# Four transfers by column quarter for the other branch's rows and the output rows

## The chip, the cores and the metric

The kernel runs on one core of a Trainium2 chip. The metric is device time in microseconds of one execution, from the timed runs. The engines are named as in the profile: PE (TensorE, with PEld for its weight loads), DVE (VectorE), ACT (ScalarE), POOL (GpSimd) and SP, the queue that issues nearly all transfers. Sixteen DMA engines move what SP issues.

## What is computed

The reference mixes two branches of one input x (2048 rows of 640) with a gate per row. Branch A goes through x in 64 segments of 32 rows; each carries a memory of 8 rows, which are the first 8 output rows of the attention of the segment before. Branch B is a gated feed-forward layer. Cut to what matters:

```python
for s in range(n_seg):                      # 64 segments, 32 heads of 192
    h = concatenate([mem, x_segment])       # 8 + 32 rows
    q, k, v = h @ Wq, h @ Wk, h @ Wv
    p = softmax(where(mask, q @ k.T * scale, -1e9))
    o = (p @ v) @ Wo
    mem = o[:, :8]; outs.append(o[:, 8:])
a = concatenate(outs)
b = (gelu(x @ w_gate) * (x @ w_up)) @ w_down
g = sigmoid((x * gate_w).sum(-1))
return g * a + (1 - g) * b
```

The memory makes the 64 segments a serial chain.

## The kernel before

The kernel has two stages. The first, up to about 185 us of the span, computes branch B in four blocks of 512 rows, writes its rows as bf16 to a scratch tensor in DRAM (`b_scr`), and loads most of branch A's weights into on-chip memory. The second, the chain, runs the 64 segments.

A segment is written as an ordered list of items (`PROG`): projections of q, k and v in groups (`g`), transposes, scores, softmax, the product with v, and the output projection (`wo`). The 32 heads are handled as four octets. The chain uses a shift: the 32 rows that a segment treats as its own are the 8 memory rows and 24 of x; the last 8 rows of x, the "left" rows, are worked on ahead in groups of four segments. A segment's output projection gives 32 rows, 24 output rows and the next memory. All 32 go through `mix` and are written by `out_store`; the last 8 places of each segment are written again by `outl_store`, with the left rows' results, which go through `mix_left` once in four segments. This makes s % 4 matter: the work on left rows differs between the four.

Not all weights fit on chip. Some pieces share a place with a partner (`partner`, `swap_in`), and in each segment 17 pieces are loaded over their partners (`swap_loads`, issued in `load_piece`, L597): in this order one Wk, four Wq, four Wk, five Wv and three Wo. Each waits on SP until PE has used the piece that stood there, and PE waits for each when it needs it. Of Wv and Wo they are those needed at the end of the segment.

The scheduler (`_Sched`) takes operations in program order and gives each engine its stream in that order. It knows which regions of memory, by bytes and partitions, an operation reads and writes, and puts a semaphore wait where an operation on another engine, or a transfer, has to be done first. A transfer adds 16 to its own semaphore when all of it has landed. An operation names a wait for every transfer that it directly depends on, unless its engine has already waited for that value.

In the chain all small transfers are on SP (`AUXQ = "sp"`), in order with the weight loads. In a segment SP issues: the nine Wk and Wq loads, four Wv loads, the store of the previous segment's output rows (`out_store`, L951), the load of the next x columns (`x_load`, L704), the fifth Wv load, three Wo loads, the load of the next q and k of left rows (L932), and then the load of branch B's rows for the current segment (`bz_load`, L942). Some segments add the load or the store of left rows (`bzl_load`, L947; `outl_store`, L956), of left x columns (L708), and the store of q and k of left rows (`left_store`, L893).

The buffer `bz` has 128 partitions of 160 elements: partitions 32j to 32j + 31 hold the 32 rows of column quarter j. There is one such buffer. `bz_load` fills it, `mix` multiplies it by 1 - g on GpSimd (L968) and adds g times the branch A result on VectorE (L970), and `out_store` writes it out in the next segment. So `bz_load` waits until `out_store` has landed, and `mix` waits for `bz_load`.

The left rows' buffer `bzl` is laid out the same way, and already goes in four transfers by column quarter:

```python
def bzl_load(g):
    for j in range(4):
        S_.add(AUXQ, lambda e, j=j: e.dma_start(bzl[32 * j:32 * j + 32], rows(b_scr, g)[1][:, :, DJ * j:DJ * (j + 1)]),
               reads=..., writes=[r_bzlj[j]], dma_sem="bzl%d" % j, name="bzl load g%d" % g)
```

At the end SP waits for all stores (`emit_final_waits`).

Of the kernel before, what the change touches and what calls it, by code (L numbers as in the profile page):

```python
# [231 lines left out]
def _build(nc, A_x, A_mem0, A_Wq, A_Wk, A_Wv, A_Wo, seg_len, w_gate, w_up, w_down,  # L232
           gate_w, out, opts=None):
# [5 lines left out]
    L = int(seg_len)  # L239
# [3 lines left out]
    DJ = Dm // 4  # L243
# [23 lines left out]
    S_ = _Sched(nc)  # L267
    Rg = S_.region
    AUXQ = opts.get("auxq", "act")

    x2 = A_x[0]
    out2 = out[0]
    b_scr = nc.dram_tensor("ffn_b_scratch", (S, Dm), BF, kind="Internal").ap()
# [63 lines left out]
    wsB_off = {}  # L337
# [14 lines left out]
    def bview(o, nbytes, plo=0, phi=128):  # L352
        return arena[plo:phi, o // 2:(o + nbytes) // 2]
# [4 lines left out]
    def sreg(o, nbytes, plo=0, phi=128):  # L358
        return Rg("sb", o, o + nbytes, plo, phi)
# [57 lines left out]
    bz, bzl = [bview(wsB_off[nm], DJ * 2) for nm in ("bz", "bzl")]  # L417
# [4 lines left out]
    zsum = fview(wsB_off["rows"], DJ * 4)  # L422
    r_zp = sreg(wsB_off["rows"], 2 * DJ * 4)
    r_bz, r_bzl = [sreg(wsB_off[nm], DJ * 2) for nm in ("bz", "bzl")]
    r_Z = [Rg("z", i, i + 1) for i in range(2)]
    mem0r = bview(wsB_off["uTl"], Dm * 2)
    r_mem0r = sreg(wsB_off["uTl"], Dm * 2)
# [206 lines left out]
    def load_residents(cls, pick=lambda key: True):  # L634
        for key in first:
# [7 lines left out]
           reads=[r_ident], writes=[r_ident])  # L643
    def asel(ap, reg, pattern, base, cm, fill):
# [12 lines left out]
           reads=[r_elw], writes=[r_elw])  # L657
# [19 lines left out]
    for h in range(NH):  # L677
        for w_, sb_, rw_, nm in ((w_gate, wg_sb, r_wg, "wg"), (w_up, wu_sb, r_wu, "wu")):
            S_.add("sp", lambda e, h=h, w_=w_, sb_=sb_: e.dma_start(
                sb_[h], w_.rearrange("(p k) f -> p k f", p=128)[:, :, FH * h:FH * (h + 1)]),  # L680
                writes=[rw_[h]], dma_sem="%s%d" % (nm, h))
# [179 lines left out]
    AUXQ = "sp"  # L861
# [48 lines left out]
    for n, (g, o) in enumerate(units):  # L910
# [7 lines left out]
        if g == 0:  # L918
            S_.add("pool", lambda e, o=o, b=b: e.tensor_copy(out=stg[:, o], in_=lst[b][:, 0]), reads=[r_lst[b]], writes=[r_stg[o]],
                   name="stg s0 o%d" % o)  # L920
# [18 lines left out]
               name="Kl s%d o%d" % (s, o))  # L939

    def bz_load(s):
        S_.add(AUXQ, lambda e: e.dma_start(bz, b_scr[L * s:L * s + L, :].rearrange("t (j n) -> j t n", j=4)),  # L942
               reads=[Rg("dr", 128 * (s // 4), 128 * (s // 4) + 128)], writes=[r_bz], dma_sem="bz", name="bz load s%d" % s)

    def bzl_load(g):
        for j in range(4):
# [1 line left out]
                   reads=[Rg("dr", 128 * g, 128 * g + 128)], writes=[r_bzlj[j]], dma_sem="bzl%d" % j, name="bzl load g%d" % g)  # L948

    def out_store(s):  # L950
        S_.add(AUXQ, lambda e: e.dma_start(out2[L * s:L * s + L, :].rearrange("t (j n) -> j t n", j=4), bz),  # L951
               reads=[r_bz], writes=[Rg("do%d" % j, s, s + 1) for j in range(4)], dma_sem="outs", watch=True, name="out s%d" % s)

    def outl_store(g):
        for j in range(4):
# [309 lines left out]
    def segment(s):  # L1265
# [3 lines left out]
        for n, item in enumerate(PROG):  # L1269
            kind, i = item[0], item[1]  # L1270
            if kind == "g":
# [8 lines left out]
                if kind == "k" and i == 1:  # L1280
                    if s > 0:
                        out_store(s - 1)
                    if s + 1 < NSEG:
                        x_load(s + 1)
# [44 lines left out]
            if n == nqkv:  # L1329
                bz_load(s)  # L1330
                if q == 2:
                    bzl_load(g)
                if q == 1 and g + 2 < NG:
                    xl_load(g + 2)
# [22 lines left out]
    for s in range(NSEG):  # L1357
        segment(s)
    out_store(NSEG - 1)
    outl_store(NG - 1)  # L1360

# [28 lines left out]
def bass_gated_mix__memory_aug_recurrent_mem_tr__glu_gated_geglu__prompt_kernel(  # L1390
    nc,
    A_x,
    A_mem0,
    A_Wq,
    A_Wk,
    A_Wv,
    A_Wo,
    A_seg_len,
    B_x,
    B_w_gate,  # L1400
    B_w_up,
    B_w_down,
    gate_w,
    out,
):
    _build(nc, A_x, A_mem0, A_Wq, A_Wk, A_Wv, A_Wo, A_seg_len, B_w_gate, B_w_up, B_w_down, gate_w, out)
# [33 lines left out]
```

## Time and profile before

| what | value |
|---|---|
| three timed runs | 1785.28, 1790.60, 1790.21 us (median 1790.21) |
| span of the profiled execution | 1783.4 us |
| other time of that execution | none is given |
| PE busy | 1629.5 us, 91% of the span |
| DVE, ACT, POOL busy | 957.7, 793.8, 319.8 us |
| moved by DMA | 524.33 MB, mean 294 GB/s |
| share of the 16 DMA engines, SP's queue | 79.5% |
| granted clock of TensorE | 0.998 |

The span is the time from the first to the last instruction on the core. A line of the profile names the source line, the engine, the operation and output<-input. Waits are told as "who waited <- for whom: us in total, times, longest". A timeline line has start, duration, engine, line, and in brackets the idle time before it and what ended it. A transfer is issued by SP ("SPq") in some tenths of a microsecond and lands later; it has landed for its users when the last DMA engine that carries part of it is done.

### The profile page before, as it was taken

The numbers are of one execution on the slowest core, as the hardware profiler recorded it, in microseconds if no ns is written. First come the engines' busy times: TensorE is split into PE (matmuls) and PEld (weight loads), VectorE is DVE, ScalarE is ACT, GpSimd is POOL, SyncE is SP. The second block draws the span as 40 slices with busy tenths as digits, with TensorE's granted clock in tenths as the row PEclk, the third lists the DMA queues.
The fourth block names the chain that finished last, engine by engine and source line by source line (L and its number), as shares of the span: only waits on it lengthen the run. The fifth ranks groups of instructions, "written<-read, shape, count | busy, mean of one in ns | idle before, by whom it ended". The sixth has DMA issues, their size and how long they took to land.

```text
span 1783.4 us, 80070 instructions
## 1 busy us (share of the span) xinstructions
PE 1629.5 (91%) x39162; PEld 817.9 (46%) x31501; DVE 957.7 (54%) x2932; ACT 793.8 (45%) x1835; POOL 319.8 (18%) x1099
## 2 busy tenths in 40 slices
PE   9999989899998999899899999899999989899987
PEld 4554444454444444454444444454444444454443
DVE  2223555555555655555565655555555655555554
ACT  3222444444444444444444444444444544444443
POOL 1100111111211111111111111111211111111211
PEclk9999999999999999999999999999999999999999
DMA  9815887888788887888788887888888887888786
GB/s 332 297 45 177 329 318 266 324 322 316 289 295 298 318 311 261 318 318 315 287 299 299 311 319 263 322 310 319 298 299 300 317 290 269 321 313 321 289 303 260
DMA packets 263390, 524.33 MB, mean 294 GB/s; under 512 B 97384, under 2 KB 116224, under 8 KB 263040
## 3 DMA queue, kind: packets, MB, share of 16 engines
q1 hardware_dynamic: 259912, 516.11, 79.5%
q8 instruction: 276, 4.52, 1.0%
q10 hardware_dynamic: 3128, 3.09, 0.5%
q14 instruction: 74, 0.61, 0.1%
HBM read 498.00 MB, written 21.11 MB: 291 GB/s over the span
## 4 chain that ended last, share of the span: by engine, by line
PE 69%; DMA 13%; DVE 8%; ACT 6%; issue 4%; SPq 0%; DVEq 0%; ACTq 0%
PE ps L1039 20%; PE ps L226 15%; PE ps L1201 8%; DMA arena<-in_A_Wv_dram 7%; PE ps L1172 3%; DMA left_qk_scratch<-arena 3%; PE ps L802 3%; PE ps L799 3%; PE ps L882 3%; DVE arena L889 3%; PE ps L1093 2%; PE ps L817 2%; ACT arena L887 2%; PE ps L1080 2%; PE ps L1088 2%
## 5 line engine op out<-in xcount | busy, mean ns | idle before, releaser
L1039 PE MATMUL ps<-arena 128*32 128x384 bf16 x9940 | 734.8, 328 | 58.5 <-DVE arena L1344 40.4
L226 PE MATMUL ps<-arena 128*32 128x384 bf16 x7680 | 584.4, 326 | 10.8 <-ACT arena L887 6.1
L1039 PEld LDWEIGHTS ps<-arena 128*32 128x32 bf16 x9940 | 254.0, 96 | 420.1 <-issue 244.4
L1073 DVE STREAM_TRANSPOSE arena<-arena 128x384 bf16<-128x384 bf16 x512 | 279.0, 564 | 227.0 <-ACT arena L1059 226.6
L1059 ACT ACTIVATE arena<-ps 128x384 bf16<-128x384 f32 x512 | 236.2, 489 | 176.3 <-PE ps L1039 164.4
L1201 PE MATMUL ps<-arena 128*32 128x320 bf16 x6144 | 297.0, 300 | 16.1 <-issue 15.5
L1201 PEld LDWEIGHTS ps<-arena 128*32 128x32 bf16 x6144 | 163.6, 97 | 75.7 <-issue 26.5
L1119 ACT ACTIVATE ps<-ps 104x160 f32<-104x160 f32 x256 | 74.3, 290 | 236.4 <-DVE ps L1109 236.4
L1107 DVE TENSOR_REDUCE arena<-ps 104x4 f32<-104x160 f32 x256 | 83.1, 325 | 176.0 <-PE ps L1093 175.7
L1157 ACT ACTIVATE arena<-ps 128x448 bf16<-128x448 f32 x192 | 104.8, 546 | 143.3 <-PE ps L1144 143.3
L1191 POOL COPY arena<-arena 128x96 bf16<-128x96 bf16 x256 | 68.4, 267 | 522.6 <-ACT arena L1183 419.3
L936 POOL COPY arena<-arena 128x96 bf16<-128x96 bf16 x256 | 70.0, 274 | 498.7 <-PE ps L1093 436.3
L1183 ACT ACTIVATE arena<-ps 128x480 bf16<-128x480 f32 (+1 forms) x256 | 138.1, 540 | 34.0 <-PE ps L1174 29.0
L1062 ACT ACTIVATE arena<-ps 128x384 bf16<-128x384 f32 x256 | 124.8, 488 | 52.7 <-PE ps L1039 52.4
L1172 PE MATMUL ps<-arena 128*64 128x160 bf16 x1536 | 122.1, 243 | 10.4 <-issue 3.4
L1172 PEld LDWEIGHTS ps<-arena 128*64 128x64 bf16 x1536 | 80.6, 109 | 97.9 <-ACT arena L1157 46.6
L882 PE MATMUL ps<-arena 128*32 128x384 bf16 x1280 | 111.1, 330 | 1.2 <-issue 1.2
L1174 PE MATMUL ps<-arena 128*64 128x64 bf16 x1536 | 105.1, 194 | 5.8 <-issue 5.8
L1121 DVE TENSOR_REDUCE arena<-ps 104x4 f32<-104x160 f32 x256 | 81.8, 320 | 51.6 <-ACT ps L1119 43.9
L889 DVE STREAM_TRANSPOSE arena<-arena 128x384 bf16<-128x384 bf16 x128 | 73.8, 577 | 57.4 <-ACT arena L887 52.6
L1224 PE MATMUL ps<-arena 128*32 128x160 bf16 x3072 | 77.1, 234 | 22.2 <-DMA arena<-in_A_Wo_dram 12.6
L887 ACT ACTIVATE arena<-ps 128x384 bf16<-128x384 f32 x128 | 62.4, 490 | 67.6 <-DVE arena L889 38.5
(84 smaller groups left out, 1816.7 us busy)
## 6 DMA issues: line engine op xcount, KB each, us to landing
arena<-in_A_Wk_dram SPq DMA_DIRECT2D x335, 384.0 KB, 7.7
arena<-in_A_Wv_dram SPq DMA_DIRECT2D x335, 384.0 KB, 9.4
arena<-in_A_Wq_dram SPq DMA_DIRECT2D x272, 384.0 KB, 5.6
arena<-in_A_Wo_dram SPq DMA_DIRECT2D x205, 480.0 KB, 7.4
left_qk_scratch<-arena SPq DMA_DIRECT2D x64, 192.0 KB, 2.6
arena<-left_qk_scratch SPq DMA_DIRECT2D x63, 192.0 KB, 7.8
ffn_b_scratch<-arena ACTq DMA_DIRECT2D x16, 160.0 KB, 3.7
arena<-ffn_b_scratch SPq DMA_DIRECT2D x64, 40.0 KB
```

Of the source, the lines that this page charges most:

```text
L226: return e.add_instruction(mybir.InstMatmult(name=nm, start_tensor_calc=like["start"], stop_tensor_calc=stop, tile_size=(128, 32), tile_po ...
L882: fns.append(lambda e, outp=outp, rhs=rhs, j=j: e.matmul(outp, lhs, rhs, start=(k == 0), stop=(k == KT - 1), tile_position=(0, 32 * j)))
L889: S_.add("dve", lambda e: e.transpose(out=dst[:, :, m].rearrange("p q c i -> p c q i"), in_=rowl.rearrange("p (c r) -> p c r", r=L)), read ...
L1039: fns.append(lambda e, outp=outp, rhs=rhs, j=j: e.matmul(outp, lhs, rhs, start=(k == 0), stop=(k == KT - 1), tile_position=(0, 32 * j)))
L1059: S_.add("act", lambda e, m=m, bk=bk: e.activation(out=rows_sb[m], in_=ps[:, bk, 0:384], func=ACTF.Copy), reads=[r_ps[bk]], writes=[r_rows ...
L1062: S_.add("act", lambda e, i=i, bk=bk: e.activation(out=v_sb[i % NVB].rearrange("p (c n) -> p c n", c=3), in_=ps[:, bk, 0:384].rearrange("p ...
L1073: S_.add("dve", lambda e: e.transpose(out=dst[:, :, 0:L], in_=rows_sb[m].rearrange("p (c r) -> p c r", r=L)), reads=[r_rows[m]], writes=[r ...
L1157: S_.add("act", lambda e: e.activation(out=PT, in_=ps[:, bank, 0:PTW + 128], func=ACTF.Copy), reads=[r_ps[bank]], writes=[r_PT], name="pT ...
L1172: return [lambda e: e.matmul(full, v[:, e0:e0 + 64], PTm[:, i], start=True, stop=False, tile_position=(0, 64 * i), skip_group_check=True), ...
L1174: lambda e: e.matmul(part, vl[:, e0:e0 + 64], PTl[:, i], start=False, stop=True, tile_position=(0, 64 * i), skip_group_check=True)]
L1183: S_.add("act", lambda e: e.activation(out=apx(u[:, 0, 0, :], [[R, na], [3 * R, 4], [1, R]]), in_=ps[:, A, 0:na * W].rearrange("p (c t r) ...
L1201: fns.append(lambda e, i=i, t=t, j=j, gv=gv: e.matmul(ps[32 * j:32 * j + 32, bank, 0:2 * DJ].rearrange("p (h n) -> p h n", h=2), lhs2[i], ...
```

## The change

The load of branch B's rows and the store of the output rows were one transfer each, over all four column quarters: the DRAM side was walked as quarter, row, column. They become four transfers each, one per quarter, with 32 rows of 160 elements on both sides. Each of the four has a region of its own (32 partitions) and a semaphore of its own, so each load waits for the store of its own quarter alone. The bytes and the rows are the same.

```diff
+    r_bzj = [sreg(wsB_off["bz"], DJ * 2, 32 * j, 32 * j + 32) for j in range(4)]
...
     def bz_load(s):
-        S_.add(AUXQ, lambda e: e.dma_start(bz, b_scr[L * s:L * s + L, :].rearrange("t (j n) -> j t n", j=4)),
-               reads=[Rg("dr", 128 * (s // 4), 128 * (s // 4) + 128)], writes=[r_bz], dma_sem="bz", name="bz load s%d" % s)
+        for j in range(4):
+            S_.add(AUXQ, lambda e, j=j: e.dma_start(bz[32 * j:32 * j + 32], b_scr[L * s:L * s + L, DJ * j:DJ * (j + 1)]),
+                   reads=[Rg("dr", 128 * (s // 4), 128 * (s // 4) + 128)], writes=[r_bzj[j]], dma_sem="bz%d" % j,
+                   name="bz load s%d" % s)
...
     def out_store(s):
-        S_.add(AUXQ, lambda e: e.dma_start(out2[L * s:L * s + L, :].rearrange("t (j n) -> j t n", j=4), bz),
-               reads=[r_bz], writes=[Rg("do%d" % j, s, s + 1) for j in range(4)], dma_sem="outs", watch=True, name="out s%d" % s)
+        for j in range(4):
+            S_.add(AUXQ, lambda e, j=j: e.dma_start(out2[L * s:L * s + L, DJ * j:DJ * (j + 1)], bz[32 * j:32 * j + 32]),
+                   reads=[r_bzj[j]], writes=[Rg("do%d" % j, s, s + 1)], dma_sem="outs%d" % j, watch=True, name="out s%d" % s)
```

The order of instructions on all engines stays as it was; SP issues eight transfers in place of two per segment. In the built program `mix`'s multiply on GpSimd waits on the four load semaphores in place of one, and its second part on VectorE, which named none of them before, names all four.

## The prediction

> **What bounds the kernel now.** I read the page first, then the waits of TensorE, the waits and the timeline of the DMA-issuing queue SP in one segment, then VectorE and GpSimd at the segment's end. The page:
>
> ```profile
> span 1783.4 us, 80070 instructions
> PE 1629.5 (91%) x39162; PEld 817.9 (46%) x31501; DVE 957.7 (54%) x2932; ACT 793.8 (45%) x1835; POOL 319.8 (18%) x1099
> PE 69%; DMA 13%; DVE 8%; ACT 6%; issue 4%; SPq 0%; DVEq 0%; ACTq 0%
> arena<-ffn_b_scratch SPq DMA_DIRECT2D x64, 40.0 KB
> ```
>
> PE carries the chain, DMA comes second with 13%. The load to be split (last line) moves only 40 KB, 64 times. The waits of PE's weight loads say which transfers PE waits for (total us, times, longest):
>
> ```profile
> PEld ps L1039 <- DMA arena<-in_A_Wv_dram: 22.2, 36, 1.8
> PEld ps L1224 <- DMA arena<-in_A_Wo_dram: 17.6, 24, 1.1
> PEld ps L1039 <- DMA arena<-in_A_Wk_dram: 12.1, 25, 1.0
> ```
>
> They are the swapped weight pieces. SP's timeline in a segment with s % 4 = 2 (start, us, line):
>
> ```profile
> 834.73 2.13 SPq L597 DMA_DIRECT2D arena<-in_A_Wv_dram  x4
> 836.90 0.57 SPq L951 DMA_DIRECT2D out_dram<-arena  x1
> 837.52 1.30 SPq L704 DMA_DIRECT2D arena<-x_scratch  x1
> 838.86 0.79 SPq L597 DMA_DIRECT2D arena<-in_A_Wv_dram  x1
> 842.62 2.18 SPq L597 DMA_DIRECT2D arena<-in_A_Wo_dram  x3
> 844.85 0.43 SPq L932 DMA_DIRECT2D arena<-left_qk_scratch  x1
> 847.08 0.55 SPq L942 DMA_DIRECT2D arena<-ffn_b_scratch  x1
> ```
>
> The stretch 835.5 to 847.9 of it (busy us of PE, PEld, DVE, ACT, POOL; last two columns: share of the 16 DMA engines, GB/s):
>
> ```profile
> 835.50:847.90 12.40, 11.15 (x290) 5.91 (x254) 7.65 (x24) 6.87 (x17) 1.87 (x7) 1.00 1.03 402
> ```
>
> All 16 engines are full in that stretch, and a 384 KB load takes 0.43 us to issue but about 1 us to move. Loads therefore stand in line: the fifth Wv load lands 9.3 us after its issue (median), the third Wo load 8.0. What counts for PE is the engine that finishes last, not SP's time of issue. In the trace I compared the last landing of the third Wo piece with the first weight load that waits for it: they are under 0.2 us apart in 29 of 63 segments, all with s % 4 = 1 or 2. In the others PE comes 0.2 to 2.6 us later.
>
> **The change, part by part.** (1) The store's time in the DMA engines. The last store of the run stands alone; the stretch 1778 to 1780 in forty slices:
>
> ```profile
> GB/s 0 0 0 0 0 0 0 0 0 0 0 0 13 38 58 77 77 77 77 83 77 77 77 70 19 0 0 0 164 0 0 0 0 0 0 0 0 0 0 0
> DMA packets 133, 0.05 MB, mean 25 GB/s; under 512 B 132, under 2 KB 132, under 8 KB 132
> ```
>
> That is 128 rows of 320 B and 4 completions at a flat 77 GB/s, where a full queue moved 402: one such transfer uses 4 of the 16 engines and holds them 40 KB / 77 GB/s = 0.53 us. Its DRAM pattern begins with the 4 column quarters, and the trace has 4 landings for it; the x load (L704), whose patterns begin with 128 rows, has 16. The new ones begin with 32 rows on both sides, and I take them by the x load: each engine gets 2 rows of each, 8 in all, 0.53 / 4 = 0.13 us, and four completions. The four old engines gain, the other twelve carry new work ahead of the fifth Wv load and the Wo loads. Lower end 0.13 us (completions free); upper end from the 10 KB loads of L947, whose last landings are 0.19 us apart where their 8 rows per engine take 0.13, so 0.06 for each further transfer: 0.13 + 4 x 0.06 = 0.37. I take 0.18, near the low end, because the completions are only 4-byte packets that the trace gives 9 ns each. It counts only where the last engine is among the twelve. The store's own four landings tell: they end a median of 0.9 us before the last landing of the x load queued right behind it, and are within 0.25 us of it in 6 of 64. So the last engine is nearly always another, and 29 segments pay: 29 x 0.18 = 5.2 us (ends 29 x 0.13 = 3.8 and 29 x 0.37 = 10.7). The Wv waits fall in the same segments and add nothing.
>
> A rule of the Trainium skill bears on this: "DMA: Bandwidth & Descriptors", "Why a DMA increments its semaphore by 16 and not by 1", says that a transfer uses the largest number of engines up to 16 that divides the slowest dimension of both its patterns. By it 4 and 128 give 4 now, and 32 and 32 give 16. The trace agrees for before (the quarter share above); no run shows the after yet. That page's "Rules for kernel authors" speak against a split: of two transfers to separate partition halves they say "Don't bother", since the parts share the same engines. By it the change gains nothing and the time is 1790 at best; no run here shows it yet.
>
> (2) SP's issues: six more per segment. A small transfer takes 0.43 (L932), 0.55 (L942), 0.58 (L951) or 0.60 us (L947), so with 0.04 between them three more are 1.4 to 1.9 us; I take 1.8. After the store they push the x load, the fifth Wv load and, if SP is still busy, Wo. Ahead of Wo SP idles 2.8 to 2.9 us (medians in segments 1 and 2, least 1.4), and the two pushed loads stand 5 us in line, so the cost is nothing; without the line each would land 1.8 us later. GpSimd's x copy comes 1.3 us after that load's landing; 0.2 is hidden.
>
> (3) The b load at the segment's end. SP already waits there for the store:
>
> ```profile
> SPq L942 <- DMA out_dram<-arena: 72.1, 44, 3.0
> ```
>
> The store will end with the last of 16 engines, not of 4: 0.9 + 0.2 us later, then 1.8 for issues. Behind it stand the bzl or left-x loads, then the next segment's q/k store and Wk, Wq loads. SP idles before these 5.8, 6.0, 3.5 and 8.4 us (s % 4 = 0, 1, 2, 3), 2.5 at the least; 2.8 is covered, barely so in one class. Where b is needed:
>
> ```profile
> 828.43 0.69 POOL L968 TENSOR_SCALAR arena<-arena 128x160 bf16<-128x160 bf16 x1 [0.81 <-DMA arena<-ffn_b_scratch]
> 830.31 0.32 POOL L936 COPY arena<-arena 128x96 bf16<-128x96 bf16 x1 [1.19 <-DVE arena L1344]
> 830.17 0.34 DVE L970 SCALAR_TENSOR_TENSOR arena<-arena 128x160 bf16<-128x160 bf16 x1
> 832.18 0.58 DVE L1073 STREAM_TRANSPOSE arena<-arena 128x384 bf16<-128x384 bf16 x1 [1.67 <-ACT arena L1059]
> ```
>
> By the line of queued loads b lands 0.5 to 1 us later. GpSimd's multiply ends 1.05 us before VectorE uses it at 830.17, and VectorE then has 1.67 us idle; GpSimd's next copy has 1.19 us and is read by the scores at 833.28. Cost nothing; without cover, at most 1 us in 64 segments.
>
> (4) More waits: mix1 on GpSimd waits on four b semaphores rather than one, mix2 on VectorE on four it did not name before. mixl1 (L976) has four such waits and starts 0.16 us after its predecessor, mix1 0.13 with one. Hidden in the same idle time.
>
> (5) The tail. The last stores of left rows start at 1780.02, on the landing of the store of 1777.41. Four issues put the last quarter's landing some 1.3 us later; the last of the four left stores waits for it, and now issues at 1780.8. Between 0 and 0.9, I take 0.5.
>
> **Sum.** 5.2 + 0.5 = 5.7 us. The profiled execution's span of 1783.4 becomes 1789.1. The page gives no other time of it; it is 1.9 us under the fastest timed run and 6.8 under the median, and I add the same 5.7 to the median: 1790.2 + 5.7 = 1796 (0.32%).
>
> **Rivals.** *SP becomes late.* Place: the end of segments with s % 4 = 2, 16 of them, with 3.5 us of cover. The store's later end takes 1.1, so it decides once a new issue takes over 0.76 us. The x load's reached 1.30 in the lines above, and 1.75 at most, for it; the rows of 0.43 to 0.60 speak against. At 1.0 each SP is 3 x 1.04 + 1.1 - 3.5 = 0.7 us late: 11 us more, 1807. *The four engines were the brake.* If the last landing is on one of the four, it moves forward by 0.53 - 0.18 = 0.35 us: 29 x 0.35 = 10 us, 1780. It decides where one of them ends more than 0.18 us after every other. For it: all four carry both small transfers, the bzl and outl quarters too. Against: the landing order in (1). *Hidden.* If PE's delay of 0.18 us is taken back by a later wait, or the new transfers hold four engines as the old ones do, 1790 to 1791. For it: half the segments have over 0.2 us to spare; against: the third Wo piece feeds the last matmuls before the next segment's rows.
>
> **How the numbers follow.** Forecast 0.50, SP late 0.22, four engines 0.14, hidden 0.14. About 0.3% (5.4 us) is what a measurement can tell from no change. The forecast's own range is 1794 to 1801, two thirds of it over 1795.6: slower 0.33 + 0.22 = 0.55; same 0.17 + 0.13 = 0.30; faster 0.14 + 0.01 = 0.15. The range runs from 1782, inside the four engines' case, to 1810, past SP's price at 1.0 us; some 0.15 is outside.
>
> **What would show it.** Right: the third Wo load's landing 0.2 us later against its issue order, PE's waits on Wo some 5 us more in total, GpSimd's wait for b longer without PE's waits on L1344 growing. SP's rows for the new transfers should read 0.43 to 0.6; at 0.8 or more the first rival holds, and PE's waits on Wk and Wq grow. If Wo and Wv waits shrink, the four engines were the brake. Wrong outright: new transfers that still hold only some engines.

## The result, and the profile after

The changed kernel took 1799.08 us (median of 20 runs), the kernel before 1789.99 us beside it: a ratio of 1.0039 by the means of the runs, interval 1.0024 to 1.0053, or +7.0 us (4.3 to 9.5; the medians alone are 9.1 us apart). A second comparison on another chip gave 1.0052 (1.0038 to 1.0066), +9.3 us. The forecast was +5.7 us, with "slower" as the likeliest outcome. The size holds; the way to it holds only in part.

The page after, on the lines shown of before, and the line of SP's queue (packets, MB, share of the DMA engines), whose line of before stands last:

```profile
span 1795.2 us, 80668 instructions
PE 1635.5 (91%) x39181; PEld 815.8 (45%) x31501; DVE 963.4 (54%) x2932; ACT 794.6 (44%) x1835; POOL 319.8 (18%) x1099
q1 hardware_dynamic: 267592, 516.14, 79.5%
PE 63%; DMA 19%; DVE 8%; ACT 5%; issue 4%; SPq 1%; DVEq 0%; ACTq 0%; POOL 0%; POOLq 0%
q1 hardware_dynamic: 259912, 516.11, 79.5%
```

The engines execute the same instructions, and DMA has gone from 13% to 19% of the chain. VectorE is busy 5.7 us longer; 3.6 us of it are mix's second part, whose mean went from 0.348 to 0.404 us. SP's queue has 267592 - 259912 = 7680 packets more. All are 4-byte completions: 64 segments x 2 transfers x (4 x 16 in place of 4). So each new transfer uses all 16 engines, which was an assumption. It is what the Trainium skill, "DMA: Bandwidth & Descriptors", "Why a DMA increments its semaphore by 16 and not by 1", gives for 32 rows on both sides.

PE's waits for the weights (lines moved by 1 to 4 in the changed file: L1039 is L1043, L1224 is L1228):

```profile
PEld ps L1043 <- DMA arena<-in_A_Wv_dram: 26.1, 49, 1.8
PEld ps L1043 <- DMA arena<-in_A_Wk_dram: 23.9, 48, 1.9
PEld ps L1228 <- DMA arena<-in_A_Wo_dram: 21.3, 27, 1.2
```

Wo has 3.7 us more, as forecast in kind. Wk, at 12.1 before, has 11.8 us more, which was not forecast (another pair of profiles, below, does not repeat it). SP's timeline where s % 4 = 2:

```profile
836.83 2.35 SPq L598 DMA_DIRECT2D arena<-in_A_Wv_dram  x4
839.22 2.87 SPq L955 DMA_DIRECT2D out_dram<-arena  x4
842.13 0.42 SPq L705 DMA_DIRECT2D arena<-x_scratch  x1
842.60 0.43 SPq L598 DMA_DIRECT2D arena<-in_A_Wv_dram  x1
844.92 1.28 SPq L598 DMA_DIRECT2D arena<-in_A_Wo_dram  x3
846.25 1.28 SPq L933 DMA_DIRECT2D arena<-left_qk_scratch  x1
849.83 1.72 SPq L944 DMA_DIRECT2D arena<-ffn_b_scratch  x4
...
856.05 0.38 SPq L894 DMA_DIRECT2D left_qk_scratch<-arena  x1
```

The four stores of this segment took longer than most: 2.87 us, where the median is 2.10. Even so SP has idle time ahead of the Wo loads and of the q/k store, so SP did not become the bound here. What did change is in VectorE's waits (before, then after):

```profile
DVE arena L970 <- POOL arena L968: 0.6, 2, 0.4
DVE arena L974 <- POOL arena L972: 21.1, 32, 2.5
```

Mix's second part on VectorE, which waited for GpSimd 0.6 us in total before, waits 21.1 us in 32 segments. One of these segments has s % 4 = 0. First VectorE, GpSimd and SP of it after the change, from their timelines:

```profile
1005.87 0.29 DVE L1348 STREAM_TRANSPOSE arena<-arena 128x96 bf16<-128x96 bf16 x1
1007.20 0.47 DVE L974 SCALAR_TENSOR_TENSOR arena<-arena 128x160 bf16<-128x160 bf16 x1 [1.03 <-POOL arena L972]
1007.59 0.57 DVE L890 STREAM_TRANSPOSE arena<-arena 128x384 bf16<-128x384 bf16 x1
...
1006.38 0.68 POOL L972 TENSOR_SCALAR arena<-arena 128x160 bf16<-128x160 bf16 x1 [1.72 <-DMA arena<-ffn_b_scratch]
...
1008.18 0.39 SPq L894 DMA_DIRECT2D left_qk_scratch<-arena  x1
1008.61 0.50 SPq L598 DMA_DIRECT2D arena<-in_A_Wk_dram  x1
```

Then a segment of the same kind in the kernel before:

```profile
804.38 0.29 DVE L1344 STREAM_TRANSPOSE arena<-arena 128x96 bf16<-128x96 bf16 x1
804.60 0.34 DVE L970 SCALAR_TENSOR_TENSOR arena<-arena 128x160 bf16<-128x160 bf16 x1
804.86 0.57 DVE L889 STREAM_TRANSPOSE arena<-arena 128x384 bf16<-128x384 bf16 x1
...
805.46 0.38 SPq L893 DMA_DIRECT2D left_qk_scratch<-arena  x1
805.89 0.50 SPq L597 DMA_DIRECT2D arena<-in_A_Wk_dram  x1
```

From the start of the last transpose of the memory rows to the first Wk load it takes 1.5 us before and 2.7 us after. The segment of before is typical; that of after is one of the three latest of its kind, with the q/k store 2.0 us behind the transposes' end where the median is 1.0. GpSimd waits for b; VectorE's mix waits for GpSimd; the transposes of the left rows stand behind mix on VectorE; the store of their q and k waits for these; and on SP the next segment's Wk and Wq loads stand behind that store. That chain became theory M. The forecast's own step, the store's extra time on every DMA engine, is theory E.

### The profile page after: what moved, and what is told of

It reads as the page before. It is cut to its first block, busy times and chain, and to the rows that moved or that the text cites. A ratio compares the mean times of both kernels' runs of the same rounds, so it can differ in the third digit from the quotient of the medians.

```text
span 1795.2 us, 80668 instructions
## 1 busy us (share of the span) xinstructions
PE 1635.5 (91%) x39181; PEld 815.8 (45%) x31501; DVE 963.4 (54%) x2932; ACT 794.6 (44%) x1835; POOL 319.8 (18%) x1099
## 3 DMA queue, kind: packets, MB, share of 16 engines
q1 hardware_dynamic: 267592, 516.14, 79.5%
## 4 chain that ended last, share of the span: by engine, by line
PE 63%; DMA 19%; DVE 8%; ACT 5%; issue 4%; SPq 1%; DVEq 0%; ACTq 0%; POOL 0%; POOLq 0%
PE ps L1043 18%; PE ps L226 13%; PE ps L1205 7%; DMA arena<-in_A_Wk_dram 6%; DMA left_qk_scratch<-arena 5%; DMA arena<-in_A_Wv_dram 5%; PE ps L800 3%; PE ps L803 3%; PE ps L1176 3%; DVE arena L890 2%; PE ps L818 2%; PE ps L1097 2%; PE ps L883 2%; DMA arena<-in_A_Wo_dram 2%; PE ps L1228 2%
## 5 line engine op out<-in xcount | busy, mean ns | idle before, releaser
L1043 PE MATMUL ps<-arena 128*32 128x384 bf16 x9940 | 737.3, 329 | 63.5 <-DVE arena L1348 39.6
L1043 PEld LDWEIGHTS ps<-arena 128*32 128x32 bf16 x9940 | 253.3, 96 | 436.7 <-issue 246.5
L1205 PE MATMUL ps<-arena 128*32 128x320 bf16 x6144 | 292.8, 299 | 12.4 <-issue 12.2
L1228 PE MATMUL ps<-arena 128*32 128x160 bf16 x3072 | 77.6, 234 | 25.8 <-DMA arena<-in_A_Wo_dram 15.8
```

What stands on the lines that cost most here:

```text
L1043: fns.append(lambda e, outp=outp, rhs=rhs, j=j: e.matmul(outp, lhs, rhs, start=(k == 0), stop=(k == KT - 1), tile_position=(0, 32 * j)))
L1205: fns.append(lambda e, i=i, t=t, j=j, gv=gv: e.matmul(ps[32 * j:32 * j + 32, bank, 0:2 * DJ].rearrange("p (h n) -> p h n", h=2), lhs2[i], ...
L1228: S_.add("pe", [lambda e, j=j, c=c, g_=g_, p=p: e.matmul(ps[32 * j:32 * j + 32, OB2, SC:512], u[:, p % 4, c, 0:L], g_[:, c, DJ * j:DJ * (j ...
```

## The experiments

All ratios are to the kernel before, run beside the others of its group on the same chip. The group of each is given, since the chip differs between groups. A difference between two rows has the uncertainty of both: by these intervals some 4 to 5 us either way.

| kernel | group | ratio (95% interval) | us, of 1790 |
|---|---|---|---|
| both split (the change) | 0 | 1.0039 (1.0024 to 1.0053) | +7.0 |
| both split, again | 2 | 1.0052 (1.0038 to 1.0066) | +9.3 |
| store alone split | 1 | 1.0011 (0.9993 to 1.0029) | +2.0 |
| load alone split | 1 | 1.0045 (1.0028 to 1.0061) | +8.1 |
| both split, left rows first | 1 | 0.9991 (0.9975 to 1.0007) | -1.6 |
| before, 0.36 us more on all engines | 1 | 1.0083 (1.0059 to 1.0108) | +14.9 |
| before, left rows first | 2 | 0.9980 (0.9965 to 0.9994) | -3.6 |
| load alone split, left rows first | 2 | 0.9999 (0.9979 to 1.0018) | -0.2 |
| before, mix late where s % 4 = 0 | 3 | 1.0013 (0.9997 to 1.0030) | +2.3 |
| before, mix late where s % 4 = 1, 2 | 3 | 0.9999 (0.9981 to 1.0017) | -0.2 |
| store split, load split where s % 4 = 0 | 3 | 1.0030 (1.0014 to 1.0045) | +5.4 |
| store split, load split elsewhere | 3 | 1.0029 (1.0015 to 1.0042) | +5.2 |

Beside the times, three moments read from the traces. They are means in us from the end of the last transpose of the memory rows: b's last landing, the start of mix's second part on VectorE, and the issue of the q/k store where s % 4 = 0.

| kernel | b lands, s % 4 = 0 / 1 / 2 / 3 | mix, 0 / 1 / 2 / 3 | q/k store, 0 |
|---|---|---|---|
| before, again | -2.23 / -1.60 / -1.82 / -3.01 | -0.03 / -0.06 / -0.07 / -0.08 | 0.84 |
| both split | -0.80 / -0.47 / -0.92 / -1.85 | 0.48 / 0.56 / 0.24 / -0.06 | 1.41 |
| both split, again | -0.98 / -0.41 / -0.96 / -1.93 | 0.25 / 0.61 / 0.25 / -0.05 | 1.14 |
| store alone | -2.32 / -1.83 / -2.19 / -3.24 | -0.08 in all | 0.81 |
| load alone | -1.42 / -0.45 / -0.92 / -1.96 | 0.04 / 0.57 / 0.22 / -0.06 | 0.92 |

**The store alone and the load alone.** The first keeps the old load beside the new store, the second the old store beside the new load:

```diff
 store alone:
-        for j in range(4):
-            S_.add(AUXQ, lambda e, j=j: e.dma_start(bz[32 * j:32 * j + 32], b_scr[...]), writes=[r_bzj[j]], ...)
+        S_.add(AUXQ, lambda e: e.dma_start(bz, b_scr[L * s:L * s + L, :].rearrange("t (j n) -> j t n", j=4)), writes=[r_bz], ...)
 load alone:
-        for j in range(4):
-            S_.add(AUXQ, lambda e, j=j: e.dma_start(out2[...], bz[32 * j:32 * j + 32]), reads=[r_bzj[j]], ...)
+        S_.add(AUXQ, lambda e: e.dma_start(out2[L * s:L * s + L, :].rearrange("t (j n) -> j t n", j=4), bz), reads=[r_bz], ...)
```

Expected of the store alone:

> Only the store is split; the load stays one transfer. Theory E (the store's extra 0.18 us on every DMA engine stands ahead of the last Wv and Wo loads): the whole cost is here, +5 us, in segments with s % 4 = 1 and 2. Theory M (b arrives late; VectorE's second part of mix then waits for GpSimd, the left transposes and the q/k store behind it are late where s % 4 = 0, and with them SP's next Wk loads): part of it is here, since the load still waits for a store that now ends with the last of 16 engines; +2 to +4 us, and VectorE's mean start of mix's second part where s % 4 = 0 is 0.3 us or more after the memory transposes' end (before: -0.07; with both split: 0.48).

Expected of the load alone:

> Only the load is split; the store stays one transfer on 4 engines. Theory E: nothing, within 1 us of before, since no weight load of the segment stands behind the load. Theory M: b is late by the three more issues and by the last of 16 engines, so +1 to +4 us, with VectorE's wait for GpSimd's multiply between 2 and 15 us in total (before: under 3; both split: 21.1).

Both missed. The store cost 2.0 us (-1.3 to 5.2), under E's 5, though the interval just reaches it, and b was not late at all. The load cost 8.1 us (5.0 to 10.9; only 5 runs), where E had nothing, and over M's 1 to 4, with VectorE's wait for GpSimd where M had it:

```profile
POOL arena L971: 14.3, 31
```

This is from the view of mix's line L973 with the load alone: what ended VectorE's idle time before it (us, times). Two things follow. The load carries most of the cost. And b's lateness comes from the load itself, not from the store's later end: with the store alone split, b lands even 0.1 to 0.4 us earlier than before.

One row speaks against M. With the load alone split the q/k store is only 0.08 us later than before (0.92 against 0.84), which M prices at 15 x 0.08 = 1.2 us at most. The 8.1 us measured for this kernel are not explained by M.

**The left rows first.** Their evacuation and transposes go ahead of mix, so that the q/k store no longer waits for it; this touches only segments with s % 4 = 0:

```diff
-        mix(s)
         if "v" in lb:
             vl_evac(s + 1, octet(s + 1, 0), lb.pop("v"), "act")
         for i in post:
             left_evac(s, *i)
+        mix(s)
```

On the changed kernel:

> Both split, but the left rows' evacuation and transposes are put ahead of mix in program order, so that the q/k store on SP no longer stands behind mix's second part. Theory M: the lateness of Wk and Wq in segments with s % 4 = 1 goes, 4 to 7 us less than the changed kernel. Theory E alone: no gain beyond the 0.3 us that mix's second part takes on VectorE in 16 segments, so 0 to 4 us less at most, and PE's waits on Wk stay at some 24 us.

On the kernel before, as the control, with a second comparison of the changed kernel in the same group:

> The kernel before with the left rows' evacuation ahead of mix, as the control. Theory M (b's lateness costs through the q/k store on SP): b is not late here, so only mix's own 0.3 us on VectorE and the store's 0.3 us go in 16 segments: 0 to 5 us less than before. If it is 7 us or more faster, moving the left rows gains by itself, and the cure seen with both split says nothing on b.

> The changed kernel once more, for a profile beside the next two: 5 to 9 us more than before.

On the load alone:

> Only the load split, left rows ahead of mix. Theory M: the load's cost goes through the q/k store where s % 4 = 0, so this is within 2 us of the control with the left rows first. Rival (the load costs in another way: its waits on VectorE and GpSimd, or its place on all 16 engines): still 6 us or more above that control.

With both split the edit gains 0.48% (from 1.0039 to 0.9991, in two groups), 8.6 us, where M expected 4 to 7; on the kernel before it gains 3.6 us, as expected; on the load alone 8.2 us (1.0045 to 0.9999, in two groups). So some 5 us of the change's cost (8.6 - 3.6; by the intervals 0 to 10) go with the wait behind mix, and 0.11% to 0.19% over the control stay. The last figure, +3.4 us for the load, lies between M's 2 and the rival's 6, and its interval, some 4 us either way, covers both.

A profile of the kernel before from the same group:

> The kernel before once more, for a profile from the same chip as the other three: PE's waits on Wk 10 to 15 us in total.

This missed. The line, and that of the changed kernel in the same group:

```profile
PEld ps L1039 <- DMA arena<-in_A_Wk_dram: 20.4, 37, 1.3
PEld ps L1043 <- DMA arena<-in_A_Wk_dram: 19.4, 42, 1.6
```

The same kernel waits 12.1 us for Wk in one profile and 20.4 in another. The growth of Wk's wait in the profile after is therefore no evidence for M; on one chip there was none. The moments in the table and the timed ratios are better evidence, though a moment moves too: the q/k store's is 1.41 and 1.14 in two profiles of the changed kernel.

A comparison within the two profiles of the changed kernel does not depend on such totals. In 7 of their 30 segments with s % 4 = 0 the q/k store is issued 1.7 us or later after the transposes; in the segment behind, PE waits 1.46 us for Wk on average. In the other 23, where it is issued at 0.81 to 1.35, PE waits 0.53 us. This fits a late q/k store that reaches PE through Wk, with small lateness taken up; a queue that runs late for another reason could show the same, so it is support and not proof. Over both profiles it is 7 x 0.93 = 6.5 us, an estimate of some 3 us per run.

**More time on all DMA engines.** Two more transfers stand behind the store, each 128 rows of 448 B of a constant tile to scratch:

```diff
                         out_store(s - 1)
+                        dummy_store(s)
```

> The kernel before, with two more transfers from on-chip memory to scratch right behind the store of the output rows, 128 rows of 448 B each over all 16 engines: 16 rows per engine, some 0.36 us, and two more issues on SP. b's load and its wait stay as they were. Theory E: from the slack of the fifth Wv and third Wo loads in the trace of before, each segment loses what of 0.36 us exceeds its slack: +11 us. Rival (PE takes a delay of this size back, and only b's lateness cost time): 0 to +2 us.

The time rose by 14.9 us, interval 10.6 to 19.3, against the 11 from the slack in the trace. The last landing of the fifth Wv load behind the fourth (mean, s % 4 = 1) went from 1.10 and 1.15 us in the two profiles of before to 1.52. So the mechanism E exists, and at this dose PE does not take it back. Two things came with the dose: b landed up to 0.7 us later, though the q/k store did not move (0.83), and SP had two more issues, with 0.5 to 1.1 us of idle time (medians) left ahead of the Wo loads where s % 4 is 1, 2 or 3. With both split or the store alone the same distance is 1.21 to 1.24: the extra time of the last engine is some 0.1 us, not 0.18. At 0.1 us in 29 segments E gives 2.9 us, or 1.6 with each segment's slack ahead of the third Wo piece taken off; both agree with the store's 2.0 (-1.3 to 5.2).

**Mix late, with no transfer touched.** One more multiply by 1.0 on GpSimd (it took 0.61 us), only in some segments:

```diff
+        if s % 4 == 0:                     # the second kernel: s % 4 in (1, 2)
+            S_.add("pool", lambda e: e.tensor_scalar(out=bz, in0=bz, scalar1=1.0, scalar2=None, op0=ALU.mult),
+                   reads=[r_bz], writes=[r_bz], name="mix1b s%d" % s)
```

> The kernel before, nothing in its transfers changed. Where s % 4 = 0, GpSimd multiplies b by 1.0 once more (0.69 us) ahead of mix's second part, so that mix is late as it is with both split. Theory M: the left transposes, the q/k store on SP and the Wk and Wq loads behind it follow, 0.3 to 0.7 us in 16 segments: +4 to +9 us. Rival (lateness of mix is absorbed, the cost of the split lies elsewhere): within 2 us of before.

> The same extra multiply where s % 4 = 1 and 2, where no q/k store stands behind mix. Theory M: VectorE is idle behind mix there, within 2 us of before although 32 segments are late. Rival (late mix costs wherever it is): +8 us or more.

Where s % 4 = 0 it cost 2.3 us, less than expected, but the q/k store was only 0.12 us later on average (0.96 against 0.84): 15 x 0.12 = 1.8 us, since the last of the 16 segments has no such store. Elsewhere it cost nothing, with mix 0.2 us later. This fits a price of lateness where the q/k store stands behind mix; but the interval (-0.5 to 5.4 us) reaches down to no change, and only one of these stores came later than 1.0 us (at 1.84), so the experiment gave too small a dose to show the price. Where s % 4 = 1 and 2 the dose was small as well.

**The load split in some segments only.** The store is split everywhere; `bz_load` takes its old form where the condition fails:

```diff
     def bz_load(s):
+        if not (s % 4 == 0):               # the second kernel: if not (s % 4)
+            S_.add(AUXQ, lambda e: e.dma_start(bz, ...rearrange("t (j n) -> j t n", j=4)), writes=[r_bz], dma_sem="bz", ...)
+            return
         for j in range(4):
```

> The store is split everywhere, the load only where s % 4 = 0. Theory M: nearly the whole cost of the change is here, +5 to +9 us. Rival: a quarter of the load's cost and the store's 2 us, +3 to +4 us.

> The store is split everywhere, the load only where s % 4 is not 0. Theory M: no more than with the store alone, 0 to +4 us. Rival (the load costs wherever it is late): +6 us or more.

The load in the 16 segments with s % 4 = 0 costs 5.4 - 2.0 = 3.4 us, 0.21 us in each, with the q/k store 0.36 us later (1.20). The load in the other 48 costs 5.2 - 2.0 = 3.2 us, 0.07 us in each, where M has nothing. With the store's 2.0 the parts sum to 8.6 us, against the 7.0 and 9.3 measured for the whole. The store's 2.0 is from another group, so each of the two differences is uncertain by some 4 us, and neither is clear of zero. The first kernel's 5.4 us (2.5 to 8.1) is where M had it, but the interval holds the rival's 3 to 4 too; the second's 5.2 us (2.7 to 7.5) is over M's 4 and under the rival's 6, and its interval holds both.

## Why the prediction was right, and where not

**The sum.** +5.7 us forecast, +7.0 measured, and slower, by 0.39% (0.24% to 0.53%). The parts were another mixture: the store, forecast at 5.2, costs some 2 (up to 5.2 by its interval); the load, forecast at nothing, some 5 to 8 (7.0 - 2.0; 8.1 alone). That the sum came out near is luck: one term too large and one put at nothing offset each other.

**(1) The store in the DMA engines** was right in mechanism and too large. The new transfers use all 16 engines, the fifth Wv and third Wo loads land later, and the dummy shows that such a delay reaches the time. The term mis-sized is 0.18 us on the last engine; the landings show some 0.1, under its lower end of 0.13. It was also charged in full to all 29 segments with under 0.2 us of slack; less each one's slack, 0.18 us gives 3.9 us and not 5.2. PE's waits on Wo, forecast to grow by some 5 us, grew by 3.7 and 3.5 in the two pairs of profiles.

**(2) SP's issues** cost nothing, as forecast. The price of a new issue was put between 0.43 and 0.60 us; the median is 0.42 to 0.43, the mean 0.53 for a store and 0.47 for a load, since some take 1 us and more. Four stores take 2.10 us together (median), four loads 1.73, so three more issues cost 1.5 and 1.2 us, under the 1.8 taken. The rival "SP becomes late" has no ground at its place: the idle time ahead of the q/k store where s % 4 = 2 is 1.2 us (median; 0.48 at the least), and ahead of Wo the medians are 1.3 to 3.0, though in 4 of 63 segments there is none.

**(3) The b load** is the step that failed. It said that b lands 0.5 to 1 us later and that this costs nothing. b lands 1.1 to 1.4 us later where s % 4 = 0 or 3 and 0.9 to 1.2 where 1 or 2, and mix waits in 32 segments. For s % 4 = 1 the 1.67 us of idle VectorE was the right cover; the reading was made on such a segment. Where s % 4 = 0, VectorE's next work is the left rows' transposes, and behind these SP's q/k store and the Wk loads. The step counted SP's idle time ahead of that store, but not that the store itself waits for VectorE behind mix. "Cost nothing" was taken from one class of segment for all four. What the runs showed in its place is that wait, by estimates of some 3 us (the Wk waits behind the 7 late stores) to 5 us (the left rows first). It does not cover all that the load costs.

**(4) More waits** did not delay mix's start: where b is early, it starts at -0.05 or earlier with its new waits as without them. But mix's second part itself got longer, from a median of 0.343 us to 0.376 with the store alone split and 0.384 with the load or both; that is 0.04 us, and what it costs was not tested. **(5) The tail** was put at 0.5 us and cost nothing: from mix's second part in the last segment to the end it took 6.45 and 6.21 us in the two profiles of before, 6.46 and 6.35 after.

**The other rivals.** "The four engines were the brake" is out: the store alone does not gain. "Hidden" is out for the whole by the interval; for the store alone it is not excluded.

**Still open** is why the load costs some 3 us where s % 4 is not 0, if it does, and 8.1 us when it alone is split. Mix is up to 0.6 us late there, three times the dose of the experiment that found no cost, so lateness is not excluded; nor is the load's place on all 16 engines at the segment's end. GpSimd's next copies also start later (0.54 us after the transposes' end where s % 4 = 1, against 0.13), but PE waits for them only once, 0.2 us, so that way is small. The lengths of the segments by class cannot decide: between two profiles each is uncertain by some 0.5 us, and 3 us are 0.07 in each. Loading b earlier into a second buffer would part the two; it wasn't tried.

The control with the left rows first has the lowest ratio here, 0.9980 (0.9965 to 0.9994) of before: it takes mix out of the way of the q/k store without touching a transfer.

## What to carry to other kernels

When a transfer gets later, follow what stands behind its user on that user's engine, and then behind that on the next queue, in every class of iteration and not in one sample. A small transfer on few DMA engines can land earlier than the same bytes in four transfers over all 16: the parts wait for the last of more engines, and the later ones are issued later. And the spread one puts its time in front of every transfer that is queued behind it (here some 0.1 us on the last engine), so on a full queue a split can cost bandwidth time even where its issues are free.

## What the runs showed of the hardware

A transfer of 32 rows of 320 B on 16 engines was cheaper to issue than one of the same size on 4 (L947): 0.42 to 0.43 us against 0.60, by the medians. The two issues behind the store also got shorter, the x load's median from 0.57 to 0.42 us and the fifth Wv load's from 0.79 to 0.43; with the load alone split, the store still on 4 engines, they stay at 0.57 and 0.79. So six more transfers cost SP less than six issues.

The 16 engines are far from even: one Wv load landed on its first engine 8.4 us after issue and on its last 11.4; the median of such a spread is 1.9 us over the chain's weight loads. So b, 40 KB that move in 0.53 us or less, landed 0.9 to 1.4 us later in four parts. Not all of that is the spread: with the load alone split, the first quarter was issued 0.2 us later than the whole load before and landed 0.4 us later (means over all segments), and the last quarter was issued 1.8 us later and landed 1.0 us later, all against the end of the memory rows' transposes.
